# Ten long and three short token blocks instead of twelve long ones, with the freed rooms given to expert weights

## The chip, the cores and the metric

The kernel runs on one core of one Trainium2 chip. The metric is device time in microseconds (us) of one execution. Memory sizes here are in KB and MB of 1024; the profile's MB and GB/s are decimal.

## What is computed

The reference chains three parts over 4608 tokens (8 sequences of 576, 512 features): a retention attention (causal scores with a decay per head, no softmax), a gated feed-forward layer and a soft mixture of experts with 32 slots.

```python
scores = scale * q @ k.T                      # per batch and head
x = ((scores * Dmat) @ v)                     # tokens x 512
h = x @ w_in                                  # 512 -> 2048
x = (h * sigmoid(1.702 * h)) @ w_out          # 2048 -> 512
logits = x @ phi                              # 32 slots
d = softmax(logits, over tokens)
slot_input = d.T @ x                          # 8 experts x 4 slots
slot_out[e] = relu(slot_input[e] @ w1[e]) @ w2[e]
out = softmax(logits, over slots) @ slot_out
```

w1 and w2 are 16 MB each.

## The kernel before

**Blocks.** The tokens come in 36 chunks of 128. Attention makes one chunk per step (`step_of`, steps 0 to 35). Everything behind it works on blocks of NB = 384 tokens, three steps each: 12 blocks, 0 to 11. The attention output x of a block is held as two float32r halves (a high part made by ScalarE in `x_high`, a low part made by GpSimd in `x_low`).

**One block.** For each of 16 groups fc of 128 hidden channels, `expert_scores` (L368) makes hp with 12 matmuls: four pieces of 128 features, three products of halves each, a 128x128 weight load before each. ScalarE applies the gate (`gelu`, L378) into gT, which keeps four groups per tile in a ring of three tiles in `gate_room`. w_out is never applied to tokens: the logits come from gT and Wp = w_out @ phi, four groups at a time (`logits_group`, L419, Lg), and the slot sums collect d.T @ gT. For these the gates must have tokens on the partitions: VectorE transposes 32x32 pieces into `pre` (`turn_fc`, L394), and 16 DMAs per half block move them into `nat` (`shuffle`, L412), 96 KB each in runs of 1 KB. The softmax over tokens is kept up from block to block: `softmax_split`, `softmax_exp` (with the matmul lt, L432), `softmax_turn` (dp, L461) and `slots_part` (Sg, L479) for block n run inside block n+1, at the groups that tables like EXP_AT name.

**The last blocks.** Block 10 (`early`) runs the last three attention steps at its groups 0, 3 and 6. Then the attention's memory is closed and becomes the pool `pw2`. Block 11 (LAST) has no block behind it: its gates are turned by TensorE (`last_turn`, L401, tpg) and copied to `nat`, without DMAs, and its softmax runs in `tail()` in one serial chain. At its group 1 an exponential and four VectorE sums finish the softmax over slots for all earlier tokens (`combine_part`).

**The tail.** After the last slot sum, w_out is applied to the 32 slots (si_ps, L682), then the first expert layer (h_ps, L710), the second (so_ps, L753 and L761), and the results are made, copied out and written (op, L787; copies L796; DMA L797), 9 MB in 12 DMAs.

**The weights' plan.** `prefetch(place)` takes the next unit of w_out (4 MB), w1 and w2 (less 1.5 MB that are kept from early on), 34.5 MB in all, and issues its load into a room of 1 MB (or 0.5 MB) whose old content is no longer needed. In block 10 it fills 1 MB of `ring` (group 2), 4 MB of `pw2` (group 6) and at the end 1.5 MB each of x and pre; in block 11 each pair of used input weights (1 MB, every second group) and some more; in the tail and in the expert layers whatever comes free (`refill`). All DMAs, loads, shuffles and results, are issued in program order by SP, on one queue; an issue that has to wait holds all behind it. The order of each engine's work is the order of the program (`manual_schedule`).

Of the kernel before, what the change touches and what calls it, by code (L numbers as in the profile page):

```python
# [31 lines left out]
NBLK = NT // NB  # L32
LAST = NBLK - 1
# [5 lines left out]
NW2 = 4  # L39
# [6 lines left out]
STEPS = NB // CP  # L46
# [87 lines left out]
def tile_kernel(ctx, tc, qkv, w_in, w_turned, w_out, phi, w1, w2, consts, out):  # L134
# [818 lines left out]
```

## Time and profile before

| | |
|---|---|
| time, median of 3 runs | 649.25 us (648.83 to 650.72) |
| the profiled execution | 650.49 us |
| its span, first to last instruction | 648.6 us |
| mean granted TensorE clock | 0.994 of full speed |
| TensorE matmuls, busy | 626.7 us, 97% |
| moved by DMA | 150.64 MB, mean 232 GB/s |

The profile is that of one execution; all its times are inside the span, which starts with the first instruction. PE is TensorE, PEld its weight loads, DVE VectorE, ACT ScalarE, POOL GpSimd, SP the engine that issues the DMAs. L368 is line 368 of the kernel. The ends of matmuls are modelled, so a busy TensorE need not be at its peak rate; the starts are measured.

### The profile page before, as it was taken

The page shows a single profiled execution, that of the slowest core. Times are in us where ns is not written, and L with a number is a line of the kernel's source. Part 1 is how long each engine was busy: PE and PEld are TensorE (multiplying, and loading weights), DVE is VectorE, ACT ScalarE, POOL GpSimd, SP SyncE. Part 2 cuts the span into 40 slices and gives each one's busy share as a digit, 9 for nine tenths or more (in the row PEclk, how much of TensorE's full clock was granted, in tenths as well). Part 3 has the DMA queues.
Part 4 walks back from the last instruction along what each step waited for, and adds up shares of the span by engine and source line. Part 5 has one row for each costly group of instructions (what it writes and reads, how often), then busy time and mean ns, then how long its engine had stood idle before and what let it go on. Part 6 is the DMA issues. An engine that isn't in the chain of part 4 may idle for free.

```text
span 648.6 us, 19162 instructions
## 1 busy us (share of the span) xinstructions
PE 626.7 (97%) x8439; PEld 538.0 (83%) x8439; DVE 293.8 (45%) x581; ACT 216.7 (33%) x409; POOL 77.6 (12%) x70
## 2 busy tenths in 40 slices
PE   6999999999999999999999999999999999999994
PEld 6898788898998989989989979989898798874562
DVE  4989933364453443454534534544535323123043
ACT  2765432141242232422412412412424224231042
POOL 2011101211112101121111011111121100001000
PEclk9999999999999999999999999999999999999997
DMA  8997657687676756746657657566566777999998
GB/s 337 404 329 267 256 109 218 164 215 187 174 265 165 195 187 163 211 141 180 172 163 182 183 145 187 170 158 179 179 176 190 251 204 209 413 361 421 412 414 353
DMA packets 62546, 150.64 MB, mean 232 GB/s; under 512 B 8192, under 2 KB 42368, under 8 KB 53248
## 3 DMA queue, kind: packets, MB, share of 16 engines
q1 hardware_dynamic: 62464, 149.43, 72.8%
q8 instruction: 66, 1.08, 0.7%
q14 instruction: 16, 0.13, 0.1%
HBM read 101.16 MB, written 13.63 MB: 177 GB/s over the span
## 4 chain that ended last, share of the span: by engine, by line
PE 87%; DMA 6%; DVE 3%; ACT 1%; issue 1%; POOL 0%; SPq 0%; DVEq 0%; ACTq 0%
PE hp L368 56%; PE Lg L419 5%; PE Sg L479 4%; PE Sp L227 4%; PE St L227 4%; DMA early_raw<-in_moe_w_in_dram 3%; PE Op L227 2%; PE h_ps L710 2%; PE op L787 2%; PE so_ps L761 1%; DMA early_raw<-in_w_turned_dram 1%; PE so_ps L753 1%; DMA ring<-in_w_turned_dram 1%; DMA pack<-in_qkv_dram 1%; PE tpg L401 1%
## 5 line engine op out<-in xcount | busy, mean ns | idle before, releaser
L368 PE MATMUL hp<-x,w 128*128 128x384 f32 x2304 | 420.0, 339 | 1.6 <-POOL x L257 1.3
L368 PEld LDWEIGHTS hp<-x,w 128*128 128x128 f32 x2304 | 397.4, 188 | 20.2 <-issue 15.7
L394 DVE STREAM_TRANSPOSE pre<-gT 128x384 f32<-128x384 f32 x172 | 95.3, 569 | 165.5 <-ACT gT L378 154.5
L378 ACT ACTIVATE gT<-hp 128x384 f32<-128x384 f32 x188 | 91.1, 490 | 232.6 <-PE hp L368 232.2
L257 POOL TENSOR_TENSOR x<-xs,x 128x512 fp32r<-128x512 f32 x33 | 42.5, 1288 | 310.6 <-ACT x L252 310.6
L227 PE MATMUL Op<-pack 64*64 64x64 f32 x2176 | 71.8, 220 | 0.2 <-issue 0.2
L227 PEld LDWEIGHTS Op<-pack 64*64 64x64 f32 x2176 | 66.8, 135 | 0.6 <-issue 0.6
L252 ACT CAST x<-xs 128x512 fp32r<-128x512 f32 x36 | 22.3, 620 | 87.5 <-DVE xs L245 87.4
L233 POOL TENSOR_TENSOR pack<-pack,cs 128x512 f32<-128x512 f32 x30 | 32.2, 1072 | 126.9 <-DMA pack<-in_qkv_dram 111.3
L227 PE MATMUL Sp<-pack 64*64 64x64 f32 x1152 | 41.3, 222 | 5.6 <-DMA pack<-in_qkv_dram 5.5
L227 PEld LDWEIGHTS Sp<-pack 64*64 64x64 f32 x1152 | 37.8, 138 | 8.1 <-DMA pack<-in_qkv_dram 5.5
L237 DVE TENSOR_TENSOR pack<-Sp,cs 128x512 f32<-128x512 f32 x36 | 24.7, 686 | 33.5 <-PE Op L227 25.8
L227 PEld LDWEIGHTS St<-pack 64*64 64x64 f32 x1024 | 33.2, 137 | 7.4 <-issue 7.3
L227 PE MATMUL St<-pack 64*64 64x64 f32 x1024 | 37.4, 224 | 0.0
L419 PE MATMUL Lg<-gT,Wp 128*32 128x384 f32 x376 | 36.3, 493 | 0.5 <-DVE Lall L466 0.5
L479 PE MATMUL Sg<-nat,dn 128*32 128x512 f32 x264 | 30.4, 593 | 0.0
L245 DVE TENSOR_TENSOR xs<-Op,cs 128x512 f32<-128x512 f32 x36 | 24.5, 681 | 3.1 <-PE Op L227 3.1
L241 DVE TENSOR_TENSOR pack<-St,cs 128x512 f32<-128x512 f32 x32 | 21.8, 680 | 3.4 <-PE St L227 2.0
L304 ACT ACTIVATE early_raw<-early_raw 128x512 f32<-128x512 f32 x28 | 18.9, 685 | 12.3 <-DMA early_raw<-in_moe_w_in_dram 6.3
L479 PEld LDWEIGHTS Sg<-nat,dn 128*32 128x32 f32 x264 | 8.4, 110 | 17.1 <-issue 16.9
L485 DVE SCALAR_TENSOR_TENSOR acc<-acc,corr,Sg 128x512 f32<-128x512 f32 x10 | 7.5, 748 | 28.1 <-PE Sg L479 28.1
L419 PEld LDWEIGHTS Lg<-gT,Wp 128*32 128x32 f32 x376 | 9.6, 109 | 11.9 <-issue 9.1
(142 smaller groups left out, 386.8 us busy)
## 6 DMA issues: line engine op xcount, KB each, us to landing
pack<-in_qkv_dram SPq DMA_DIRECT2D x36, 1024.0 KB, 6.2
nat<-pre SPq DMA_DIRECT2D x352, 96.0 KB, 2.2
wx<-in_moe_w_dram SPq DMA_DIRECT2D x19, 1024.0 KB, 11.2
ring<-in_moe_w_out_dram SPq DMA_DIRECT2D x16, 512.0 KB, 4.0
early_raw<-in_moe_w_in_dram SPq DMA_DIRECT2D x15, 512.0 KB, 6.7
early_raw<-in_w_turned_dram SPq DMA_DIRECT2D x13, 512.0 KB, 6.9
wx<-in_moe_w_dram SPq DMA_DIRECT2D x11, 512.0 KB, 10.1
out_dram<-wx SPq DMA_DIRECT2D x5, 1024.0 KB, 7.5
```

The costliest lines, as they stand in the source:

```text
L227: pe.matmul(o[oh, p, j, :], w[h, a, p, j], w[h, b, p, j], start=first_, stop=True, skip_group_check=True)
L233: (dve if n in (3, 4) else pool).tensor_tensor(k, k, by_state(ksc[:, n % NPB, :]), op=ALU.mult)
L237: dve.tensor_tensor(packs[n][:, SC], Sps.pop(n), across(dtab), op=ALU.mult)
L241: dve.tensor_tensor(packs[n][:, SS], St[n // NPB], by_state(stsc[:, n % NPB, :]), op=ALU.mult)
L245: dve.tensor_tensor(xss[g], Ops.pop(g), across(osc), op=ALU.mult)
L252: act.copy(xh[b_][:, :, i * CP:(i + 1) * CP], xss[g].rearrange("p a j c -> p a (j c)"))
L257: (eng or pool).tensor_tensor(xl[b_][:, :, cols_], xss.pop(g).rearrange("p a j c -> p a (j c)"), xh[b_][:, :, cols_], op=ALU.subtract)
L368: pe.matmul(hp, wt[fc][:, a, dc, :], b[n][:, dc, :], start=(i == 0), stop=(i == 3 * NDC - 1))
L378: act.activation(gT[n, g][:, fl, :], hps.pop((n, fc)), AF.Gelu_apprx_sigmoid)
L394: dve.transpose(pre[n, hf][:, :, :, fh, :].rearrange("p c b i -> p (c b) i"), gT[n, g][:, fl, :].rearrange("p (x j) -> p x j", j=32))
L419: pe.matmul(Lg[n][32 * fl:32 * fl + 32, :], Wp[:, g * GF + fl, :], gT[n, g][:, fl, :], start=(g == 0), stop=(g == NFC // GF - 1))
L479: pe.matmul(Sg[32 * b:32 * b + 32], dn[n][:, c, :], nv[:, 4 * b:4 * b + 4], start=(c == 0), stop=(c == NT128 - 1))
```

## The change

Blocks 0 to 9 stay at 384 tokens; the last 768 tokens are cut into three blocks of 256 (10, 11 and LAST = 12) instead of two of 384. With them:

- Block 10 is now the `early` one and is short; its attention steps stand at groups 0, 4 and 8. The x of step 32 is made one step later, and that of steps 34 and 35 after the attention is closed, in a room of `pw2` (which has three weight rooms now, not four); until then their raw values lie in `gate_room`, of which short blocks use 3072 of 4608 columns.
- In the short blocks VectorE turns the gates late, from group 10 on, and all 16 groups go through one shuffle at the block's end, with runs of 2 KB and 128 KB per DMA, behind the weight loads issued there.
- Expert weights are loaded into the third of `pre` that short blocks don't use (group 2 of block 10), the free third of `gate_room` (end of block 10), the x of block 11 (its end), all of `pre_room` (group 7 of the last block) and the free part of `nat` (group 10). The old loads into `pre` at the end of block 10 and in block 11 are gone.
- In the last block the exponential for the slots stays at group 1, and the sums behind it (`combine_rest`) follow the softmax turn. In block 2's first group the eight matmuls with the high half of x stand first.

```diff
 NP = H // 2
 NB = 384
 NT128 = NB // 128
-NBLK = NT // NB
-LAST = NBLK - 1
+NLONG = 10
...
 GF = 4
 HF = NFC // 2
 NQ = 4
 DQ = DM // NQ
...
 NSTEP = NT // CP
-STEPS = NB // CP
+NSHORT = 2
+NBLK = NLONG + (NSTEP - NLONG * NT128) // NSHORT
+LAST = NBLK - 1
 PC = NP * CP
...
-EARLY_STEP_AT = {0: 0, 3: 1, 6: 2}
-EARLY_LOGITS_AT = {0: ((1, 2), (1, 3)), 8: ((0, 0), (0, 1))}
-EARLY_SPLIT_AT, EARLY_EXP_AT, EARLY_TURN_AT, EARLY_SLOTS_AT = 0, 1, 3, 8
+EARLY_STEP_AT = {0: 0, 4: 1, 8: 2}
+EARLY_LOGITS_AT = {0: ((1, 2), (1, 3)), 9: ((0, 0), (0, 1))}
+EARLY_SPLIT_AT, EARLY_EXP_AT, EARLY_TURN_AT, EARLY_SLOTS_AT = 0, 1, 4, 12
+SHORT_LOGITS_AT = {0: ((1, 2), (1, 3)), 9: ((0, 0), (0, 1))}
+SHORT_TURNS = {10: (0, 1, 2, 3), 11: (4, 5, 6, 7), 12: (8, 9), 13: (10, 11, 12), 14: (13, 14), 15: (15,)}
 LATE_TURNS = {**{fc: () for fc in range(4)}, 4: (0, 1), 5: (2, 3), 6: (4, 5), 7: (6, 7)}
-LAST_LOGITS = {0: ((1, 2), (1, 3)), 4: ((0, 0),), 8: ((0, 1),), 12: ((0, 2),)}
-LAST_TURNS = {6: (0, 1), 7: (2, 3), 8: (4, 5), 9: (6, 7), 10: (8,), 11: (9,), 12: (10,), 13: (11,)}
-LAST_EXP_AT, LAST_TURN_AT, LAST_SLOTS_AT = 1, 3, 6
+LAST_LOGITS = {0: ((1, 2), (1, 3)), 6: ((0, 0),), 9: ((0, 1),), 13: ((0, 2),)}
+LAST_TURNS = {4: (0,), 5: (1,), 6: (2, 3), 7: (4,), 8: (5,), 9: (6, 7), 11: (8, 9), 12: (10,), 13: (11,), 14: (12,)}
+LAST_EXP_AT, LAST_TURN_AT, LAST_SLOTS_AT = 1, 4, 10
 LAST_ACT = (0, 2, 4, 6, 8, 11, 13)
-NPRE = NTILE - 2 * NT128
+NPRE = NTILE - 2 * NSHORT
+
+
+
+def chunks_of(n):
+    return NT128 if n < NLONG else NSHORT
+
+
+def first_step(n):
+    return NT128 * n if n < NLONG else NT128 * NLONG + NSHORT * (n - NLONG)
+
+
+def block_of(g):
+    return max(n for n in range(NBLK) if first_step(n) <= g)
...
-    packs[2] = pb.tile([128, 6, NP, NSEQ, C], F32, tag="pre", name="pack2", bufs=2)
+    pre_room = pb.tile([128, 6 * 1024], F32, name="pre_room")
+    packs[2] = pre_room[:, 0:3072].rearrange("p (c a j d) -> p c a j d", c=6, a=NP, j=NSEQ)
...
     def scale_out(g):
-        xss[g] = pa.tile([128, NP, NSEQ, C], F32, tag="xs", name="xs")
+        if block_of(g) == LAST:
+            room = gate_room[:, 3072 + 512 * (g - first_step(LAST)):][:, :512]
+            xss[g] = room.rearrange("p (a j c) -> p a j c", a=NP, j=NSEQ)
+        else:
+            xss[g] = pa.tile([128, NP, NSEQ, C], F32, tag="xs", name="xs")
         dve.tensor_tensor(xss[g], Ops.pop(g), across(osc), op=ALU.mult)
 
+    def x_of(g):
+        n = block_of(g)
+        if n not in xt:
+            if n == LAST:
+                xt[n] = pw2.tile([128, 2, NDC, NSHORT * CP], F32R, tag="x", name="x", bufs=1)
+            else:
+                xt[n] = (pg if n % 2 else pb).tile([128, 2, NDC, NB], F32R, tag="x", name="x", bufs=1)
+        i = g - first_step(n)
+        return [xt[n][:, a, :, i * CP:(i + 1) * CP] for a in range(2)]
...
+        if first_step(NLONG + 1) < g < first_step(LAST):
+            x_high(g - 1)
+            x_low(g - 1)
         scale_out(g)
-        x_high(g)
-        x_low(g)
+        if first_step(NLONG + 1) != g < first_step(LAST):
+            x_high(g)
+            x_low(g)
         if g + 2 < NSTEP:
             load_step(g + 2)
...
-    def gate():
-        return gate_room[:, GF * NB * (next(gates) % 3):][:, :GF * NB].rearrange("p (l t) -> p l t", l=GF)
+    def gate(n):
+        w = GF * CP * chunks_of(n)
+        return gate_room[:, w * (next(gates) % 3):][:, :w].rearrange("p (l t) -> p l t", l=GF)
 
     def expert_scores(n, fc):
-        hp = hps[n, fc] = ps.tile([128, NB], F32, tag="h", name="hp", bufs=3)
-        i = 0
-        for dc in range(NDC):
-            for a, b in ((0, xh), (0, xl), (1, xh)):
-                pe.matmul(hp, wt[fc][:, a, dc, :], b[n][:, dc, :], start=(i == 0), stop=(i == 3 * NDC - 1))
-                i += 1
+        hp = hps[n, fc] = ps.tile([128, NB], F32, tag="h", name="hp", bufs=3)[:, 0:CP * chunks_of(n)]
+        terms = [(a, b, dc) for dc in range(NDC) for a, b in ((0, 0), (0, 1), (1, 0))]
+        if fc == 0 and n == 2:
+            terms.sort(key=lambda t: t[0] + 2 * t[1])
+        for i, (a, b, dc) in enumerate(terms):
+            pe.matmul(hp, wt[fc][:, a, dc, :], xt[n][:, b, dc, 0:CP * chunks_of(n)], start=(i == 0), stop=(i == 3 * NDC - 1))
...
+    def last_half(fc):
+        room = nat[LAST][:, (4096, 0)[fc // HF]:][:, :2048]
+        return room.rearrange("p (c a f i) -> p c a f i", c=NSHORT, a=4, f=HF)
+
+    def nat_of(n):
+        if n not in nat:
+            if n <= NLONG:
+                nat[n] = pm.tile([128, 6 * 1024], F32, tag="nat", name="nat")
+            else:
+                nat[n] = nat[NLONG]
+        k = chunks_of(n)
+        return nat[n][:, 0:2048 * k].rearrange("p (c a f i) -> p c a f i", c=k, a=4, f=NFC)
+
+    def pre_of(n, hf):
+        if n < NLONG:
+            room, f = pre_room[:, 3072 * (1 - hf):][:, :3072], HF
+        else:
+            room, f = pre_room[:, 0:2048 * NSHORT], NFC
+        return room.rearrange("p (c b f i) -> p c b f i", b=4, f=f, i=32)
...
     def shuffle(n, hf, rows=range(4)):
-        if n not in nat:
-            nat[n] = pm.tile([128, NT128, 4, NFC, 32], F32, tag="nat", name="nat")
+        to, of = nat_of(n), pre_of(n, hf)
+        fs = slice(hf * HF, (hf + 1) * HF) if n < NLONG else slice(0, NFC)
         for a in rows:
             for b in range(4):
-                sp.dma_start(nat[n][32 * b:32 * b + 32, :, a, hf * HF:(hf + 1) * HF, :],
-                             pre[n, hf][32 * a:32 * a + 32, :, b])
+                sp.dma_start(to[32 * b:32 * b + 32, :, a, fs, :], of[32 * a:32 * a + 32, :, b])
 
...
-        prefetch_three(pg.tile([128, 3, 1024], F32, tag="x", name="wx", bufs=1), 2)
-        prefetch(lambda: gate_room[:, 2560:])
-        halves = [gate_room[:, 1024:1536], acc]
-        dp = ps.tile([128, NT128, 128], F32, tag="L", name="dp")
-        for c in range(NT128):
+        prefetch(lambda: pw2.tile([128, 2048], F32, tag="x", name="wx", bufs=1))
...
-        free = [nat[n][:, c].rearrange("p a f i -> p (a f i)") for c in range(NT128)]
-        for c in range(NT128 - 1):
-            prefetch(lambda c=c: free[c])
-        prefetch(lambda: free[NT128 - 1][:, 1024:], 1)
+        for o in (0, 4096, 5120):
+            prefetch(lambda o=o: nat[n][:, o:o + 1024], 1)
...
-            early = n == LAST - 1
+            early, short = n == NLONG, n > NLONG
             step_at, logits_at, split_at, exp_at, turn_at, slots_at = (
                 (EARLY_STEP_AT, EARLY_LOGITS_AT, EARLY_SPLIT_AT, EARLY_EXP_AT, EARLY_TURN_AT, EARLY_SLOTS_AT) if early else
-                (STEP_AT if n < LAST - 2 else BEFORE_EARLY_STEP_AT, LOGITS_AT, SPLIT_AT, EXP_AT, TURN_AT, SLOTS_AT))
+                ({}, SHORT_LOGITS_AT, EARLY_SPLIT_AT, EARLY_EXP_AT, EARLY_TURN_AT, EARLY_SLOTS_AT) if short else
+                (STEP_AT if n < NLONG - 1 else BEFORE_EARLY_STEP_AT, LOGITS_AT, SPLIT_AT, EXP_AT, TURN_AT, SLOTS_AT))
             for fc in range(NFC):
                 main_fc(n, fc)
-                for f in LATE_TURNS.get(fc, (fc,)) if n == 2 else (fc,):
+                for f in LATE_TURNS.get(fc, (fc,)) if n == 2 else SHORT_TURNS.get(fc, ()) if n >= NLONG else (fc,):
                     turn_fc(n, f)
...
                 if fc in step_at:
-                    step_of((n + 1) * STEPS + step_at[fc], between)
+                    step_of(NT128 * (n + 1) + step_at[fc], between)
                 else:
                     between()
-                if fc == (0 if early else min(step_at)) and (early or n == 2):
+                if (fc == 0 and early) or (n == 2 and fc == min(step_at)):
                     shuffle(n - 1, 1)
                 if early and fc == 2:
                     prefetch(lambda: ring_raw[:, 0:4].rearrange("p a f -> p (a f)"))
+                    prefetch(lambda: pre_room[:, 4096:6144])
                 if early and fc == max(step_at):
                     att_ctx.close()
                     pw2 = ctx.enter_context(tc.tile_pool(name="pw2", bufs=NW2, side="right", reuse_waits="tile"))
                     for _ in range(NW2):
                         prefetch(place_in(pw2, "w", NW2))
+                    for g in range(first_step(LAST), NSTEP):
+                        x_high(g)
+                        x_low(g)
                 if fc == slots_at:
                     slots_part(n - 1)
-                    shuffle(n, 0)
+                    if not (early or short):
+                        shuffle(n, 0)
                 if fc == exp_at:
                     softmax_exp(n - 1)
                 if fc == turn_at:
                     softmax_turn(n - 1)
-                if fc == NFC - 1 and not early:
-                    if n < LAST - 2:
-                        shuffle(n, 1)
-                if fc == NFC - 1 and early:
-                    prefetch_three(pb.tile([128, 3, 1024], F32, tag="x", name="wx", bufs=1), 2)
+                if fc == NFC - 1 and n < NLONG - 1:
                     shuffle(n, 1)
-                    prefetch_three(pb.tile([128, 3, 1024], F32, tag="pre", name="wx", bufs=2), 0)
+                if fc == NFC - 1 and n >= NLONG:
+                    prefetch_three((pg if n % 2 else pb).tile([128, 3, 1024], F32, tag="x", name="wx", bufs=1), 2)
+                    if early:
+                        prefetch(lambda: gate_room[:, 3072:4096], 1)
+                    shuffle(n, 0)
                 if n == 3 and fc == 0:
                     for unit, a in zip(kept, (4, 8)):
                         load_unit(unit, lambda a=a, n=len(unit): ring_raw[:, a:a + 2 * n].rearrange("p a f -> p (a f)"))
@@ -884,24 +927,27 @@
                 softmax_split(n - 1)
             if fc == LAST_EXP_AT:
                 softmax_exp(n - 1)
-                combine_part(0, NPRE)
+                act.activation(Lall[:, 0:NPRE], Lall[:, 0:NPRE], AF.Exp)
             if fc == LAST_TURN_AT:
                 softmax_turn(n - 1)
+                combine_rest(0, NPRE)
             if fc == LAST_SLOTS_AT:
                 slots_part(n - 1)
-            if fc == 5:
-                prefetch_three(pb.tile([128, 3, 1024], F32, tag="pre", name="wx", bufs=2), 0, lone=True)
+                prefetch(lambda: nat[LAST][:, 2048:4096])
             for f in LAST_TURNS.get(fc, ()):
                 turn_fc(n, f)
-            if fc == 13:
-                prefetch(lambda: gate_room[:, 1536:2560], 1)
             if fc == 0:
-                prefetch(place_in(pw, "w1", 2, 1), 1)
+                prefetch(place_in(pw, "w1", 2, 1), 1, True)
             elif fc % 2 == 0:
                 prefetch(place_in(pw, "w", NFC // 2 - 1))
             if fc == GF:
-                gate()
-                prefetch(lambda: gate_room[:, 0:1024], 1)
+                gate(n)
+                prefetch(lambda: gate_room[:, 1024:2048], 1)
+            if fc == 7:
+                for i in range(2):
+                    prefetch(lambda i=i: pre_room[:, 2048 * i:2048 * i + 2048])
+            if fc == 14:
+                prefetch(lambda: gate_room[:, 2048:3072], 1)
         tail()
```

## Rows read from the trace of the kernel before

**Rows 1.** The page: busy engines, slices of the span, one instruction group, one DMA issue.
```profile
PE 626.7 (97%) x8439; PEld 538.0 (83%) x8439; DVE 293.8 (45%) x581; ACT 216.7 (33%) x409; POOL 77.6 (12%) x70
...
DMA  8997657687676756746657657566566777999998
GB/s 337 404 329 267 256 109 218 164 215 187 174 265 165 195 187 163 211 141 180 172 163 182 183 145 187 170 158 179 179 176 190 251 204 209 413 361 421 412 414 353
...
L394 DVE STREAM_TRANSPOSE pre<-gT 128x384 f32<-128x384 f32 x172 | 95.3, 569 | 165.5 <-ACT gT L378 154.5
...
nat<-pre SPq DMA_DIRECT2D x352, 96.0 KB, 2.2
```
**Rows 2.** The chain that ended last, 478 to 500 (start, length in us, what).
```profile
479.99 8.52 PE hp L368 x48
...
494.63 4.17 PE hp L368 x24
```
**Rows 3.** The same chain, 500 to the end.
```profile
513.93 1.43 PE Lg L419 x16
515.36 2.57 PE Sg L479 x24
517.93 16.86 PE hp L368 x96
...
551.20 2.71 PE Sg L479 x24
...
556.81 0.66 PE tpg L401 x6
...
559.55 0.78 PE Lg L419 x8
...
579.08 1.16 PE Lg L419 x8
...
580.26 0.57 DVE Lp L614
...
584.42 2.83 PE Sg L648 x24
...
607.05 1.01 PE hT_ps L716 x8
```
**Rows 4.** Stages: busy us of each engine, granted clock, DMA share, GB/s.
```profile
486.40:505.00 18.60, 18.60 (x349) 16.96 (x348) 10.05 (x22) 7.97 (x14) 3.62 (x3) 1.00 0.64 180
...
549.00:560.00 11.00, 11.00 (x81) 8.07 (x79) 1.86 (x3) 2.67 (x6) 0.00 (x0) 1.00 0.94 359
...
575.00:585.00 10.00, 8.77 (x58) 6.27 (x60) 3.74 (x12) 4.36 (x11) 0.00 (x0) 1.00 0.92 326
...
600.00:625.00 25.00, 25.00 (x372) 13.62 (x364) 4.01 (x14) 4.50 (x10) 0.00 (x0) 1.00 1.01 413
625.00:640.00 15.00, 13.97 (x240) 9.69 (x236) 8.50 (x16) 8.25 (x22) 0.00 (x0) 1.00 1.01 412
640.00:648.60 8.60, 0.02 (x1) 0.00 (x0) 0.59 (x3) 0.27 (x2) 0.00 (x0) 0.55 0.74 303
```
**Rows 5.** Timeline of SP's DMA issues, 486 to 562.
```profile
491.08 13.30 SPq L412 DMA_DIRECT2D nat<-pre  x16
...
533.94 13.22 SPq L412 DMA_DIRECT2D nat<-pre  x16
```
**Rows 6.** The same timeline, 600 to the end.
```profile
638.95 1.64 SPq L797 DMA_DIRECT2D out_dram<-nat  x2
640.69 1.14 SPq L797 DMA_DIRECT2D out_dram<-wx  x1
```
**Rows 7.** What the DMA engines moved from 549 to the end.
```profile
DMA packets 6784, 38.93 MB, mean 389 GB/s; under 512 B 754, under 2 KB 760, under 8 KB 3064
```
**Rows 8.** TensorE's waits, whole span (us in total, times, longest).
```profile
PE Lg L419 <- DVE Lall L466: 0.5, 1, 0.5
```
**Rows 9.** TensorE's waits, 100 to 125.
```profile
PE hp L368 <- POOL x L257: 0.4, 1, 0.4
```

More of the change, by code (lines that the diff above doesn't have):

```diff
@@ L38 @@
 HF = NFC // 2
-NW2 = 4
+NW2 = 3
 NQ = 4
@@ L398, in last_turn @@
         g, fl = divmod(fc, GF)
-        tp = ps.tile([128, NT128, 4, 32], F32, tag=tag, name="tpg", bufs=3)
-        for c in range(NT128):
+        tp = ps.tile([128, NT128, 4, 32], F32, tag=tag, name="tpg", bufs=3)[:, 0:NSHORT]
+        for c in range(NSHORT):
             pe.transpose(tp[:, c].rearrange("p a i -> p (a i)"), gT[n, g][:, fl, c * 128:(c + 1) * 128], ident)
@@ L485, in slots_part @@
             dve.scalar_tensor_tensor(acc, acc, st["corr"], sg, op0=ALU.mult, op1=ALU.add)
-    def combine_part(t0, t1):
-        L = Lall[:, t0:t1]
-        act.activation(L, L, AF.Exp)
-        combine_rest(t0, t1)
     def combine_rest(t0, t1):
@@ L613, in tail @@
         lg = Lg.pop(n)
-        dve.tensor_copy(Lp[:, 0], lg)
+        dve.tensor_copy(Lp[:, 0, 0:w], lg)
         turn_fc(n, 13)
-        lt = ps.tile([128, NB], F32, tag="L", name="lt")
-        pe.matmul(lt, sum4, Lp[:, 0], start=True, stop=True)
+        lt = ps.tile([128, NB], F32, tag="L", name="lt")[:, 0:w]
+        pe.matmul(lt, sum4, Lp[:, 0, 0:w], start=True, stop=True)
         late = {fc: last_turn(n, fc, "h") for fc in (14, 15)}
@@ L625, in tail @@
         dve.reduce_max(mb, lt, axis=AX.X)
-        act.copy(Lp[0:NS, 1], lt[0:NS])
+        act.copy(Lp[0:NS, 1, 0:w], lt[0:NS])
         dve.tensor_tensor(mnew, mb, st["m"], op=ALU.max)
         dve.tensor_scalar(negm, mnew, -1.0, None, op0=ALU.mult)
-        dr = ps.tile([128, NT128, NS], F32, tag="St", name="dr")
-        for c in range(NT128):
+        dr = ps.tile([128, NT128, NS], F32, tag="St", name="dr")[:, 0:k]
+        for c in range(k):
             pe.transpose(dr[:, c, :], Lp[0:NS, 1, c * 128:(c + 1) * 128], ident[0:NS, 0:NS])
@@ L640, in tail @@
-        for c in range(NT128):
+        prefetch(lambda: pw2.tile([128, 2048], F32, tag="x", name="wx", bufs=1))
+        prefetch(lambda: gate_room[:, 0:1024], 1)
+        halves = [gate_room[:, 4096:4608], acc]
+        dp = ps.tile([128, NT128, 128], F32, tag="L", name="dp")[:, 0:k]
+        for c in range(k):
             pe.transpose(dp[:, c, :], dT[:, c * 128:(c + 1) * 128], ident)
-        dn_ = pm.tile([128, NT128, NS], F32, tag="dn", name="dn")
+        dn_ = pm.tile([128, NT128, NS], F32, tag="dn", name="dn")[:, 0:k]
@@ L643, in tail @@
         dve.tensor_copy(dn_, dp[:, :, 0:NS])
         Sg = ps.tile([128, 4, 4, 32], F32, tag="r", name="Sg", bufs=3)
-        for c in range(NT128):
-            nv = nat[n][:, c].rearrange("p a f i -> p f a i")
+        for c in range(k):
             for b in range(4):
-                pe.matmul(Sg[32 * b:32 * b + 32], dn_[:, c, :], nv[:, 4 * b:4 * b + 4],
-                          start=(c == 0), stop=(c == NT128 - 1))
-        mx = pm.tile([128, NT128], F32, tag="mx", name="mx")
+                nv = last_half(4 * b)[:, c].rearrange("p a f i -> p f a i")
+                pe.matmul(Sg[32 * b:32 * b + 32], dn_[:, c, :], nv[:, 4 * (b % 2):4 * (b % 2) + 4],
+                          start=(c == 0), stop=(c == k - 1))
@@ L668, in tail @@
         NCT = cT[0].shape[1]
-        si_flat = free[NT128 - 1][:, 0:NE * (NDC * NS + SE)]
+        si_flat = nat[n][:, 1024:1024 + NE * (NDC * NS + SE)]
         pool.memset(si_flat[:, 0:NE * NDC * NS], 0.0)
```

66 lines of the change are left out of this document (28 added, 38 removed).

## The prediction

> **What bounds the kernel now.** I read the page first [rows 1]: TensorE is busy 97% of the span, and from slice 34 on the DMA engines are full as well, at 353 to 421 GB/s, where they move 107 to 270 before. So two things can set the end. The chain that ended last, read in two stretches [rows 2, 3], is TensorE throughout: groups of 12 expert matmuls (hp, one per 128 hidden channels), logits (Lg), slot sums (Sg), and from 579.08 us a serial tail in which a 384-wide softmax is passed between engines. [...] SP's own timeline and the DMA list [rows 5 to 7] then say what the DMA engines do: after 549.0 they move 38.93 MB. That is 27.5 of the 34.5 MB of weights that the plan holds (7 were issued by then), 9 MB of results and a rest, in 99.6 us. At the 0.415 MB/us of the full stretches this is 93.8 us; the other 5.8 are lost in 549-560 (1.5), 575-585 (2.1) and the run-out after 640 (2.3) [rows 4]. The queue is one line, so the results, the last of them issued at 640.7, wait behind the last weights. TensorE alone would end nearly as soon: from 638.95 SP still issues 2.25 MB [rows 6], and with an empty queue these need 5.6 us and about 1.5 to land (a 96 KB transfer takes 2.2 in all [rows 1]), 646.1, plus what follows the last landing. A DMA queue that is early can give at most 1.2 us; one that is late is paid in full.
>
> **The price of a short matmul.** [...] From the load's side: six 128-column loads with their transposes take 0.66 us, 110 each, and eight loads with only 32 columns to move 1.01 us, 126 each [rows 3]. [...]
>
> **TensorE's chain, part by part**, from block 10's start (486.4: 479.99 plus 36 of 48 matmuls [rows 2]) to the end.
> - Two blocks of 384 have 384 pairs, 66.7 us; three of 256 have 576, 69.4: **+2.7** (115.9: 0.0; 126: +5.9).
> - The last block turns its gates on TensorE, now two chunks for three: 13 groups before the tail, one 0.11 us transpose less in each [rows 3]: **-1.4**.
> - Logits cost 1.43 us for 16 matmuls together and 0.78 for 8 [rows 3]; by columns plus the start, 1.0 and 0.55. Before: three times 1.43 and three times 0.78; after: 1.43, four times 1.0, three times 0.55: **+0.5**.
> - Slot sums go by chunks, whose number stays 36; but a 2.57 us one [rows 3] and two of 1.8 now lie before the tail, where there were two of 2.57 and 2.71: **+0.9**. A third softmax before the tail adds 0.3 of small matmuls and 0.5 of switches: **+0.8**.
> - In the last block the sums over finished tokens (combine_rest) move behind the turn of the softmax, which had held TensorE 0.5 us; the shorter groups leave ScalarE's table switches less cover (three groups are now 4.3 us, not 6.3), and I give back 0.3: **-0.2**. In block 2 the matmuls with the low half go last, which covers a 0.4 us wait for GpSimd [rows 8, 9]: **-0.4**.
> - The tail shrinks from 384 to 256 columns: slot sum 2.83 to 1.97, the logits 1.16 to 0.9, and the other five steps of 0.5 to 0.9 us between 580.26 and 584.42 by a fifth to a quarter each, 0.75 in all [rows 3]: **-1.9**.
> Sum **+0.9**. Bunched transposes on VectorE (45% busy in all) and the later split of steps 32, 34 and 35 cost nothing: each still precedes its use by several groups; without that cover a transposition is about 0.4 us (0.57 at 384 [rows 1]).
>
> **The DMA queue.** Up to the end of block 11 the new order issues rooms of 1 + 1 + 3 + 1.5 + 0.5 = 7 MB, so 27.5 are still to come, as many as the old one had left at 549.0 [rows 7]. The question is when the rest begins to flow.
> - Block 10 took 46.3 us (486.4 to 532.7, the second being 517.93 plus 84 of 96 matmuls [rows 3]). With 16 groups of 1.446 for 2.086 and 0.4 less for logits it takes 35.7. Block 11 has no attention steps (6.1), shorter logits, slot sum and turns (1.4): 28.1. With block 2's 0.4 it ends at 549.8.
> - During block 11 no room comes free: what was issued at block 10's end (2 MB, and the shuffle) is done some 12 us later, and the engines stand nearly empty for some 15 us.
> - Only after its last matmul SP can issue 1.5 MB into x and then the shuffle of block 11, 16 DMAs of 128 KB, an extra one: the old order shuffled nothing after 549. A shuffle's price: 486.4-505 holds 0.64 x 18.6 = 11.9 us of DMA time, of which one 1 MB pack is 2.5, so 9.4 us for 16 DMAs with runs of 1 KB [rows 4, 5]. Now there are two thirds as many runs, of 2 KB: by runs 6.3 us, by bytes 5.1, by DMAs 9.4; I take 6.3, as 1 KB runs moved far below the full rate. SP's issue took 13.2 to 13.3 us for 16, waits included [rows 5]; 0.5 over the DMA time is my allowance, up to 3.
> - So weights flow again from 549.8 + 0.4 (SP's waits) + 3.8 + 6.3 + 0.5 = 560.8. Left are 26 MB of weights and 9 of results, with 0.1 of instructions 36.8 million bytes: 88.7 us, and the run-out 2.3: **651.8**. Before it was 648.6: **+3.2**. The extra rooms (pre_room, nat) keep the queue full from there, which is why the 3.6 us lost in 549-585 are not lost again; this is already in the sum.
> By TensorE alone the end would be 646.1 + 0.9 and what follows the landing, earlier than that; so the queue decides, +3.2. The sum stands against the profiled execution (650.49 us, 1.9 around its span), which lies 1.2 over the median 649.25; I add it to the median: **652.5 us**. Bounds: the shuffle by bytes and no allowance +1.5; 115.9 ns per pair takes 1.8 off block 11's end; SP at its old 13.3 us +5.9; 126 ns another 2.1.
>
> **The rivals.** About 0.3% (1.95 us) is what a measurement of this kernel can tell from no change: slower begins at 651.2, faster at 647.3.
> - *The queue is no later, TensorE decides.* If SP gets the weights in flight by 558 (short shuffle, a pair near 117), the queue ends as before or earlier, and the chain's +0.9 less at most 1.2 of queue leaves about 649. For it: DMA time falls by some 6 us in all with the larger runs. Against: the hole in block 11 is longer than that.
> - *Faster.* The weight load alone sets a short pair, 110 ns, as the transposes have it [rows 3]: the matmuls take 63.4 us, -3.3, the chain is -5.1, block 11 ends at 545.8, and with the shuffle at 5.1 and no allowance the flow starts at 555.1: the queue ends at 646.1, TensorE earlier, so 646.7. It decides from a flow before 556 on. [...]
> - *The load is no longer hidden.* At 126 ns the chain is +4.1 and the flow starts 2.1 later: queue +5.3, 654.6.
>
> **How the numbers follow.** The queue late as worked out 0.48 (0.42 over 651.2, 0.06 below it); TensorE decides, 0.22; faster 0.17; load exposed 0.13. So faster 0.17, within 0.28, slower 0.55. The likeliest case alone reaches from 650 to 655.5. The range of 8 in 10 takes in the no-change case and most of the faster one: 646.5 to 655.5.
>
> **What would show it.** After: hp groups of 12 at 1.45 us in blocks 10 to 12 (1.39 or 1.51 for the bounds); DMA nearly idle for 15 us before block 11's end; SP's first weights of the last block near 560; the share full from there to the end; the last weight landing near 628, 3 us later than before, while TensorE's last matmul moves by about one. Wrong it would be if the queue runs dry before the results, if the hole is filled, or if pairs come at 110.

## The result and the profile after

The changed kernel takes 659.05 us (median of 5 runs, 657.39 to 660.05), the one before 649.25 (648.83 to 650.72): ratio 1.0144, 95% interval 1.0124 to 1.0164, 9.4 us of 649. It is slower, as forecast, but by three times the 3.2 us that I worked out, and outside the range. The profiled execution took 659.09, its span 657.3, 8.7 more than before.

The page after, busy engines and slices; it answers to [rows 1].
```profile
PE 629.4 (96%) x8648; PEld 540.9 (82%) x8648; DVE 297.5 (45%) x607; ACT 222.2 (34%) x431; POOL 77.2 (12%) x70
...
PEclk9999999999999999999999999999999999999977
DMA  8987657786786647667566568476568775999998
GB/s 319 402 328 268 254 126 198 193 216 160 184 295 177 183 147 186 176 166 179 175 152 180 167 157 223 160 183 182 149 182 228 282 189 149 297 421 413 416 419 353
```
TensorE is busy 2.7 us longer, but its share of the span falls to 96%. The chain that ended last, 515 to the end, in place of [rows 3]:
```profile
544.68 5.83 PE hp L400 x48
...
581.01 1.17 PE Lg L466 x8
...
585.63 1.99 PE Sg L687 x16
...
588.83 15.13 DMA nat<-in_moe_w_dram
...
604.02 15.19 DMA wx<-in_moe_w_dram
...
619.27 14.98 DMA pre_room<-in_moe_w_dram
...
634.29 1.08 PE so_ps L798 x16
...
644.37 3.13 PE op L824 x26
```
48 short pairs take 5.83 us, 121.5 ns each. From 588.8 on three loads lie on the chain, each 15 us from issue to landing: that is the length of the queue, not of a load (1 MB takes 2.5 us at 415 GB/s). The stages, against [rows 4]; the last three columns are the granted clock, the DMA share (above 1 it means full) and GB/s:
```profile
534.00:549.00 15.00, 15.00 (x134) 12.71 (x133) 6.03 (x16) 3.08 (x8) 0.00 (x0) 1.00 0.32 70
549.00:556.00 7.00, 7.00 (x67) 6.28 (x67) 1.94 (x7) 3.94 (x9) 0.00 (x0) 1.00 0.81 260
556.00:562.00 6.00, 5.77 (x52) 5.12 (x51) 4.10 (x9) 3.70 (x8) 0.00 (x0) 1.00 1.05 222
562.00:566.00 4.00, 4.00 (x37) 3.86 (x34) 0.42 (x1) 1.19 (x5) 0.00 (x0) 1.00 0.71 158
566.00:575.00 9.00, 9.00 (x79) 6.88 (x78) 2.02 (x4) 2.19 (x6) 0.00 (x0) 1.00 0.99 381
...
600.00:625.00 25.00, 23.69 (x348) 12.84 (x340) 3.54 (x12) 4.07 (x8) 0.00 (x0) 1.00 1.02 415
625.00:640.00 15.00, 10.71 (x174) 6.78 (x178) 4.17 (x10) 4.12 (x12) 0.00 (x0) 0.77 1.02 420
640.00:657.30 17.30, 6.96 (x102) 5.01 (x94) 5.41 (x12) 4.83 (x13) 0.00 (x0) 0.75 0.86 357
```
The hole of block 11 is there (0.32 from 534 to 549). Behind it comes the row to look at: from 556 to 562 the DMA engines are full (1.05) and move only 222 GB/s, where weights move at 415 to 420. That is block 11's shuffle. Only from 566 on do weights flow. SP's issues say the same, against [rows 5, 6]: the shuffle takes it from 550.04 for 14.06 us, and the next weights are issued at 564.21.
```profile
522.88 14.49 SPq L460 DMA_DIRECT2D nat<-pre_room  x16
549.14 0.81 SPq L562 DMA_DIRECT2D wx<-in_moe_w_dram  x2
550.04 14.06 SPq L460 DMA_DIRECT2D nat<-pre_room  x16
564.21 1.49 SPq L562 DMA_DIRECT2D wx<-in_moe_w_dram  x3
...
619.27 0.33 SPq L562 DMA_DIRECT2D pre_room<-in_moe_w_dram  x1
```
Two waits on TensorE are new; the granted clock falls at the time of the longer one (its mean is 0.77 of full speed from 625 to 640):
```profile
PE so_ps L798 <- DMA pre_room<-in_moe_w_dram: 4.3, 1, 4.3
PE so_ps L798 <- DMA wx<-in_moe_w_dram: 1.3, 1, 1.3
```

### The profile page after: what moved, and what is told of

The parts are those of the page before. It is cut to its first block, busy times and chain, and to the rows that moved or that the text cites. A ratio compares the mean times of both kernels' runs of the same rounds, so it can differ in the third digit from the quotient of the medians.

```text
span 657.3 us, 19648 instructions
## 1 busy us (share of the span) xinstructions
PE 629.4 (96%) x8648; PEld 540.9 (82%) x8648; DVE 297.5 (45%) x607; ACT 222.2 (34%) x431; POOL 77.2 (12%) x70
## 4 chain that ended last, share of the span: by engine, by line
PE 81%; DMA 12%; DVE 3%; ACT 1%; issue 1%; POOL 0%; SPq 0%; DVEq 0%; ACTq 0%
PE hp L400 57%; PE Lg L466 5%; PE Sg L523 5%; PE St L245 4%; PE Sp L245 4%; DMA early_raw<-in_moe_w_in_dram 4%; PE Op L245 3%; DMA wx<-in_moe_w_dram 2%; DMA nat<-in_moe_w_dram 2%; DMA pre_room<-in_moe_w_dram 2%; DMA early_raw<-in_w_turned_dram 1%; PE op L824 1%; PE so_ps L798 1%; DMA pack<-in_qkv_dram 1%; DVE w L357 1%
## 5 line engine op out<-in xcount | busy, mean ns | idle before, releaser
L400 PE MATMUL hp<-x,w 128*128 128x384 f32 (+1 forms) x2496 | 422.9, 327 | 1.5 <-POOL x L284 0.7
L409 ACT ACTIVATE gT<-hp 128x384 f32<-128x384 f32 (+1 forms) x204 | 93.7, 466 | 238.0 <-PE hp L400 237.5
L442 DVE STREAM_TRANSPOSE pre_room<-gT 128x384 f32<-128x384 f32 (+1 forms) x188 | 97.8, 542 | 157.6 <-ACT gT L409 139.1
L284 POOL TENSOR_TENSOR x<-xs,x 128x512 fp32r<-128x512 f32 x31 | 40.0, 1290 | 281.4 <-ACT x L280 281.4
L245 PE MATMUL Op<-pack 64*64 64x64 f32 x2112 | 70.1, 221 | 0.5 <-issue 0.5
L245 PEld LDWEIGHTS Op<-pack 64*64 64x64 f32 x2112 | 65.2, 135 | 0.8 <-issue 0.7
L251 POOL TENSOR_TENSOR pack<-pack,cs 128x512 f32<-128x512 f32 x29 | 30.7, 1060 | 139.5 <-DMA pack<-in_qkv_dram 133.5
L466 PE MATMUL Lg<-gT,Wp 128*32 128x384 f32 (+1 forms) x408 | 36.9, 468 | 0.9 <-DVE Wp L370 0.9
```

The lines of the kernel that those rows point to most:

```text
L245: pe.matmul(o[oh, p, j, :], w[h, a, p, j], w[h, b, p, j], start=first_, stop=True, skip_group_check=True)
L251: (dve if n in (3, 4) else pool).tensor_tensor(k, k, by_state(ksc[:, n % NPB, :]), op=ALU.mult)
L284: (eng or pool).tensor_tensor(xl, xss.pop(g).rearrange("p a j c -> p a (j c)"), xh, op=ALU.subtract)
L400: pe.matmul(hp, wt[fc][:, a, dc, :], xt[n][:, b, dc, 0:CP * chunks_of(n)], start=(i == 0), stop=(i == 3 * NDC - 1))
L409: act.activation(gT[n, g][:, fl, :], hps.pop((n, fc)), AF.Gelu_apprx_sigmoid)
L442: dve.transpose(pre_of(n, hf)[:, :, :, fh if n < NLONG else fc, :].rearrange("p c b i -> p (c b) i"), gT[n, g][:, fl, :].rearrange("p (x j ...
```

## Experiments

Three theories. **1**: the end is set by when weights flow again behind block 11's shuffle. **2**: short matmuls and TensorE's added work set it. **3**: the last weight unit comes last but is used second in the last quarter of the output; this wait and the lower clock after it set the end. Each run was timed beside the kernel before, and ratios are to that. The profiles differ by up to 3.6 us in when block 10 ends, which has nothing to do with the edits, so I also give the **rest**: the span less the time at which SP starts block 10's shuffle. For the changed kernel it is 657.3 - 522.88 = 134.4 us. A rest comes from one profile. The two pairs of runs below that differ least (e6 and e6b, e7 and e7b) have rests 0.4 and 1.4 us apart, so a difference of about 1 us in it is not shown by itself.

**Without the shuffle (e1).** The last block's slot sums then use gates that were never moved.
```
-                    shuffle(n, 0)
+                    if early:
+                        shuffle(n, 0)
```


> Leaves out the shuffle of block 11's gates (its 16 DMAs), so the last block's slot sums use gates that were never moved. Theory 1 (the end is set by when weights flow again behind that shuffle on the DMA queue): the last weight's issue moves from 619.3 us to about 605 and the kernel gains 8 to 10 us against the changed kernel, to about 649 to 651, until TensorE's chain decides. Theory 2 (256-column matmuls and TensorE's added work set the end): no change, 658 to 660. Theory 3 (the order of the last weight units, with the drop of the clock after it, sets the end): 2 to 4 us less at most, as far as the wait for them shrinks.

650.97 us, ratio 1.0014 (0.9998 to 1.0029), rest 126.3: nearly the whole loss is gone, 8.1 us by the rest. The last weight is issued at 609.0 for 619.3; I had said about 605. Theory 2 falls, since every short matmul is still there.

**Where TensorE alone would end (e9).** As e1, with `turn_fc` of block 11 left out and the two 1 MB rooms of `pre_room` loaded behind block 10's shuffle.

> Where TensorE's chain alone would end: the changed kernel without block 11's transposition and shuffle (both left out, so the last slot sums read block 10's gates), and with 2 MB of weights loaded into the room of the transposed gates in the hole of block 11, from 540 us on. TensorE's work is that of the changed kernel. If the change costs TensorE the 0.9 us that the prediction worked out and the DMA queue alone makes the rest: the DMA engines are no longer full at the end, and the time is 645 to 648, a little below that of the run without the shuffle. If TensorE's chain sets the end already there: no change against that run, 650 to 651.

650.91 us, ratio 1.0001 (0.9984 to 1.0018), rest 126.6: the second case. 2 MB loaded earlier bring nothing, and the engines have slack (share 0.64, windows of this run):
```profile
566.00:575.00 9.00, 9.00 (x79) 6.88 (x78) 1.60 (x3) 2.17 (x6) 0.00 (x0) 1.00 0.64 226
```
TensorE waits for no DMA in e1 and e9. Its last matmuls, in the kernel before, in e1 and in e9 (start and length):
```profile
636.39 3.13 PE op L787 x26
```
```profile
635.40 3.13 PE op L824 x26
```
```profile
638.68 3.13 PE op L824 x26
```
From block 10's first matmul (at 486.27, 484.01 and 487.51) TensorE's chain takes 153.2, 154.5 and 154.3 us. So e1 and e9 end with TensorE's chain, which the change made 1.1 to 1.3 us longer behind that point; by the ratio, e9 lies within -1.0 and +1.2 us of the kernel before. In these three traces the DMA engines are full from 600 to 640 (share 1.01) and the span ends 9.1 to 9.5 us behind TensorE; what a faster TensorE would gain is not shown.

**The order of the last weights (e2).**
```
-        def second_layer(q, e):
+        def second_layer(q, e, last=NE - 1):
...
-                          start=(e == 0 and f < 4), stop=(e == NE - 1 and f >= 4))
+                          start=(e == 0 and f < 4), stop=(e == last and f >= 4))
...
-        for e in range(NE):
-            second_layer(3, e)
+        for e, x in enumerate((0, 2, 3, 4, 5, 6, 7, 1)):
+            second_layer(3, x, 1)
```


> The changed kernel with the experts of the last quarter of the output in the order 0, 2, 3, 4, 5, 6, 7, 1, so that the weight unit that is loaded last is used last. Theory 1 (the DMA queue decides, and TensorE's 5.6 us of waits for weights and its lower clock behind them are hidden by the results still queued): 0 to -1 us, 658 to 659. Theory 3 (these waits and the clock set the end): -4 to -6 us, 653 to 655. Theory 2: no change.

657.47 us, ratio 1.0117 (1.0099 to 1.0136), rest 134.5, as without the edit (by the ratios 1.8 us less). The windows of this run:
```profile
634.00:640.00 6.00, 4.91 (x58) 3.48 (x46) 3.65 (x8) 3.54 (x11) 0.00 (x0) 1.00 1.03 426
640.00:645.00 5.00, 0.00 (x0) 0.00 (x0) 0.50 (x3) 0.23 (x2) 0.00 (x0) 0.62 1.01 423
645.00:655.00 10.00, 0.00 (x0) 0.00 (x0) 0.00 (x0) 0.00 (x0) 0.00 (x0) 0.50 0.82 340
```
TensorE is done by 640, at full clock; in the changed kernel it was 647.5 (644.37 and 3.13). Block 10 ends 1.7 us earlier in this profile, so the order gains TensorE about 6 us. The DMA engines still move results for 15 us, and the end stays. Theory 3 falls.

**Delay alone, in the kernel before (e3).**
```
             if fc == 0:
+                more = pd.tile([4, 128, 2, EF], F32, name="more")
+                for i in range(4):
+                    sp.dma_start(more[i], w1[i, 0])
                 prefetch(place_in(pw, "w1", 2, 1), 1)
```


> The kernel before, with 4 MB of copies from HBM to HBM put on SP's queue just ahead of the last block's first weights; nothing of the computation is left out, and TensorE's work is that of the kernel before. Theory 1: a delay of the DMA flow alone makes the loss of the change: 4 MB cost 8 to 10 us (at 2.4 us per MB, less about 1 us that the queue was early; more if a copy costs a read and a write), 657 to 660. Theory 2: the queue has slack, at most +2 us.

659.97 us, ratio 1.0156 (1.0134 to 1.0177): 10.1 us, 2.5 for each MB. The same waits of TensorE appear here, without one short matmul:
```profile
PE so_ps L761 <- DMA wx<-in_moe_w_dram: 6.9, 4, 4.3
```

**The price of the shuffle: half the bytes (e4), twice the DMAs (e8).**
```
-                sp.dma_start(to[32 * b:32 * b + 32, :, a, fs, :], of[32 * a:32 * a + 32, :, b])
+                cs_ = slice(0, 1) if n == NLONG + 1 else slice(0, chunks_of(n))
+                sp.dma_start(to[32 * b:32 * b + 32, cs_, a, fs, :], of[32 * a:32 * a + 32, cs_, b])
```
e8 instead issues one such DMA for each chunk `c`. e4 leaves the second chunk's gates unmoved.

> The changed kernel with only the first of block 11's two 128-token chunks shuffled: 16 DMAs of 64 KB for 16 of 128 KB (the second chunk's gates are not moved, so part of the last slot sums is wrong). Theory 1 with the price by bytes or runs: half of the gain of leaving the shuffle out, 4 to 5 us, 654 to 655. Theory 1 with the price by DMAs (SP's issue and its waits for landings): nearly no gain, 0 to 2 us. Theory 2: no change.

> The changed kernel with block 11's shuffle cut into 32 DMAs of 64 KB for 16 of 128 KB (the same bytes in the same runs of 2 KB); nothing is left out. If the shuffle is paid by the DMA (0.63 us of SP's issue each): the weights of the last block start about 10 us later and the kernel is 8 to 10 us slower than the changed kernel, 667 to 669. If it is paid by bytes or runs: 0 to 1 us slower, 659 to 660.

e4: 657.55 us, ratio 1.0109 (1.0091 to 1.0126), rest 133.7, only 0.7 less (2.3 by the ratios). e8: 668.95 us, ratio 1.0286 (1.0264 to 1.0308), rest 143.9, 9.4 more. SP's issues in e4, and then in e8:
```profile
549.62 13.30 SPq L461 DMA_DIRECT2D nat<-pre_room  x16
```
```profile
549.71 23.38 SPq L461 DMA_DIRECT2D nat<-pre_room  x32
```
Windows of e4:
```profile
556.00:562.00 6.00, 5.77 (x52) 4.99 (x51) 3.80 (x8) 3.40 (x8) 0.00 (x0) 1.00 0.35 81
```
With half the bytes the engines are a third busy and SP takes nearly as long as ever; e8 has 16 more DMAs of the same 64 KB than e4, and they cost 10.1 us of SP, 0.63 each. So at 64 KB a DMA costs its issue, and SP's issue alone keeps 7.4 of the 8.1 us that e1 gave back. At 128 KB both limits meet: SP's 14.1 us, and 2.1 MB / 0.222 = 9.4 us of DMA time behind 3.8 for x. These two runs can't tell whether the DMA time alone would be enough there.

**Another queue (e5), two queues (e12).**
```
-                sp.dma_start(to[32 * b:32 * b + 32, :, a, fs, :], of[32 * a:32 * a + 32, :, b])
+                (pool if n == NLONG + 1 and b % 2 else sp).dma_start(
+                    to[32 * b:32 * b + 32, :, a, fs, :], of[32 * a:32 * a + 32, :, b])
```
is e12; e5 is without `and b % 2`.

> The changed kernel with block 11's 16 shuffle DMAs issued from GpSimd's queue instead of SP's, so that SP may issue the last block's weights from 549.5 us on, beside them; nothing is left out. If SP's own issue and its waits for landings hold the flow (14 us for 16 DMAs while the DMA engines could do more): 4 to 6 us faster than the changed kernel, 653 to 655. If the DMA engines' time is what the shuffle costs (9.4 us for 16 DMAs with runs of 2 KB, whoever issues them): only the gaps of 562 to 568 us come back, 1 to 2 us, 657 to 658.

> The changed kernel with block 11's 16 shuffle DMAs split between two queues, 8 on SP's and 8 on GpSimd's, so that issuing them takes half the time and the weights follow 8 of them; nothing is left out. If SP's issue alone held the flow and the DMA engines could move the 2.1 MB at the 0.415 MB/us of weights (5 us): 4 to 6 us faster than the changed kernel, 653 to 655. If the DMA engines need 9.4 us for it whoever issues (0.222 MB/us at a full share): only the gaps come back, 1 to 2 us, 657 to 658; with TensorE waiting for the later half as in the run on GpSimd's queue alone, no gain or a loss.

e5: 665.82 us, ratio 1.0239 (1.0204 to 1.0274), rest 141.2: neither case. Weights are issued on SP's queue beside the shuffle (seven loads from 550.18 to 563.04), the DMA engines are full (1.02 from 566 to 575), the shuffle's last DMA, issued at 571.66, lands at 582, and TensorE's slot sum waits:
```profile
PE Sg L523 <- DMA nat<-pre_room: 11.0, 1, 11.0
```
e12: 657.04 us, ratio 1.011 (1.0084 to 1.0137), rest 133.6: 0.8 us by the rest, 2.2 by the ratios. With half of the issue taken from SP the engines stay full and are still slow, although the first weights (from 559.9 on) are in this window of e12:
```profile
556.00:562.00 6.00, 5.77 (x51) 4.98 (x50) 4.22 (x9) 2.76 (x8) 0.00 (x0) 1.00 1.04 236
```
SP issues the weights 2.9 us earlier than in the changed kernel, counted from block 10's shuffle, and only 0.8 to 2.2 us come of it. So at 128 KB the DMA time alone is enough for nearly the whole price, as SP's issue alone is in e4. The two limits lie within a microsecond or two of each other, and taking one away gives back no more than that. The issues of e12, on SP's and on GpSimd's queue:
```profile
548.59 11.16 SPq L460 DMA_DIRECT2D nat<-pre_room  x8
```
```profile
549.24 4.40 POOL L460 DMA_DIRECT2D nat<-pre_room  x8 [40.63 <-PE hp L400]
```

**Why half the rate: the order of the halves (e15 on one queue, e14 on two).**
```
+        if n == NLONG + 1:
+            for a in (0, 1, 2, 3):
+                for b in (0, 1):
+                    sp.dma_start(to[32 * b:32 * b + 32, :, a, fs, :], of[32 * a:32 * a + 32, :, b])
+                    x, y = (a + 2) % 4, b + 2
+                    pool.dma_start(to[32 * y:32 * y + 32, :, x, fs, :], of[32 * x:32 * x + 32, :, y])
+            return
```
is e14; e15 issues the same pairs in the same order, both on `sp`.

> The changed kernel with block 11's 16 shuffle DMAs in another order on the same queue: each one to partitions 0 to 63 is followed by one to partitions 64 to 127 (its source likewise from the other half); nothing is left out. If the shuffle's 0.222 MB/us belong to each DMA of 32 partitions by itself, or SP's issue holds it: no change, 658 to 660. If DMAs of different halves move beside each other: up to 4 us of DMA time less, but SP's issue of 14 us keeps most of it, 657 to 658. [...]

> The changed kernel with the shuffle split between two queues by halves: SP moves to partitions 0 to 63, GpSimd's queue to 64 to 127 at the same time, and from different halves too; nothing is left out. Against the split run before, where both queues went to both halves: if the halves move beside each other, the 2.1 MB take 5 to 6 us instead of 9.4 and the kernel gains 2 to 4 us more, 653 to 655. If they don't: as that run, 656 to 658. [...]

e15: 658.65 us, ratio 1.013 (1.0108 to 1.0151), rest 134.5. e14: 657.74 us, ratio 1.0125 (1.0096 to 1.0154), rest 133.3, as e12. The windows in which SP issues nothing else, of the changed kernel and then of e15:
```profile
557.50:562.00 4.50, 4.27 (x40) 3.62 (x38) 3.80 (x8) 2.22 (x7) 0.00 (x0) 1.00 1.06 223
```
```profile
557.50:562.00 4.50, 4.28 (x38) 3.90 (x41) 3.63 (x8) 2.28 (x6) 0.00 (x0) 1.00 0.99 234
```
By share that is 210 GB/s and 236, an eighth more and far from 415. The order of the halves is a small part of it; most of the low rate stays with each of these DMAs by itself. They copy within SBUF, and between two groups of 32 partitions; no run copies within SBUF over more partitions, so which of the two makes the rate low is not shown.

**Mends with nothing left out: 1 MB into the hole (e10), with two queues (e13), with the halves (e16).**
```
...
-        room = nat[LAST][:, (4096, 0)[fc // HF]:][:, :2048]
+        room = nat[LAST][:, (0, 2048)[fc // HF]:][:, :2048]
...
                     shuffle(n, 0)
+                    if early:
+                        prefetch(lambda: nat[NLONG][:, 4096:6144])
...
-                prefetch(lambda: nat[LAST][:, 2048:4096])
...
```
The weights take the last third of `nat`; the last block's gates are turned from its group 10 on, into the two thirds that block 11's gates leave then.

> The changed kernel with 1 MB loaded in the hole of block 11 and the shuffle as it is: the last third of the token-major gates takes weights right behind block 10's shuffle (537 us), and the last block's gates are turned from its channel group 10 on into the first two thirds, which the changed kernel gave to gates and to weights; nothing is left out. Theory 1: 1 MB less behind the shuffle, 2 to 2.5 us faster than the changed kernel, 656 to 657. If the bunched transposes hold TensorE up and TensorE decides: no gain or a loss of 1 us.

> The same split of the shuffle together with the 1 MB loaded in the hole of block 11 (the last block's gates turned from its channel group 10 on); nothing is left out. If both gains are of DMA time on one queue, they add: 1 to 2 us below the run with the 1 MB alone, 653.5 to 655 where that run gave 655.5. If TensorE's wait for the later half decides: equal to that run or slower.

> The split by halves together with the 1 MB loaded in the hole of block 11 (the last block's gates turned from its channel group 10 on); nothing is left out. If the halves move beside each other: 650 to 652, as much as the whole loss back, until TensorE's chain decides. If not: as the split run with the 1 MB, 654 to 655.

e10: 655.46 us, ratio 1.0075 (1.0049 to 1.0101), rest 131.4: 3.0 less, what 1 MB costs (2.5 in e3) and a little. e13: 654.36 us, ratio 1.0067 (1.0047 to 1.0086), rest 129.8. e16: 653.83 us, ratio 1.0057 (1.0038 to 1.0077), rest 129.7. Half of the loss or more comes back. The gains seem to add; the intervals of e10, e13 and e16 overlap.

**No shuffle, block 11 turned on TensorE (e6, e6b), with 3 MB in the hole (e7, e7b).** `turn_fc` takes the last block's way for block 11 too. In e6 and e7 the ninth channel group was written over block 10's gates before block 10's slot sums read them; e6b and e7b turn it one position later.

> The changed kernel with block 11's gates turned on TensorE, as the last block's are (32 transposes of 0.11 us, 3.5 us of TensorE's time, with copies on ScalarE and VectorE), in place of 16 VectorE transposes and the 16 shuffle DMAs; every weight is loaded into the same room at the same place of the order; nothing is left out. Theory 1 (the shuffle in front of the weights is the loss): the flow starts at 549.5 us and the kernel gains 7 to 9 us, 650 to 652. Theory 2 (TensorE's work sets the end): 3 to 4 us slower, 662 to 663.

> As the run before (block 11 turned on TensorE, no shuffle of its gates), and the rooms that this frees loaded in the hole of block 11: 2 MB into the room of the transposed gates as soon as block 10's shuffle has landed (540 us), 1 MB into the middle third of the token-major gates after block 10's slot sums (543 us); nothing is left out. Theory 1: 3 MB, 7 us of DMA time, move from behind 549 us into the hole, and the queue is early enough for TensorE to decide: 645 to 648, faster than both kernels. Theory 2: as the run before or slower.

> Block 11 turned on TensorE as in the run of that kind before, with the ninth of its channel groups turned only behind block 10's slot sums (one position later), so that these sums are whole; nothing is left out. As there: 653 to 655 on TensorE's chain, which the run before showed 5 us longer than without the shuffle (32 transposes and their starts), and no DMA bound in front of it.

> The same with the ninth group behind block 10's slot sums, and 3 MB loaded in the hole of block 11; nothing is left out. Theory 1 with TensorE's chain as it stood in the run of that kind before: the DMA engines have slack in the last block, and the time is that of the run without loads in the hole, within 1 us: 653 to 656.

e6: 654.61 us, rest 130.8; e6b: 654.07 us, ratio 1.0058 (1.0036 to 1.008), rest 130.4; e7: 656.0 us, rest 131.4; e7b: 656.05 us, ratio 1.0075 (1.005 to 1.0101), rest 130.0. All lie 3.7 us or more above e1 by the rest. 3 MB in the hole bring nothing: the rest moves by less than a microsecond either way, and the ratio of e7b is the higher one. The queue is relieved (share 0.67 from 566 to 575 in e7b, below), and TensorE's transposes now set the end: from block 10's first matmul to its last one TensorE takes 3.4 us longer in e6b and e7b than in e1, and 32 transposes of 0.11 us (0.66 for 6 [rows 3]) are 3.5. I had forecast e7 below both kernels; that was wrong.
```profile
566.00:575.00 9.00, 9.00 (x80) 7.38 (x72) 2.77 (x5) 2.05 (x6) 0.00 (x0) 1.00 0.67 231
```
No version beat the kernel before: by e1 and e9 TensorE's chain ends no sooner than it did.

## Why the prediction was too small

- **Pair price**: 120.5 ns forecast, 121.5 measured (5.83 us for 48). Right. The 120.5, on which the +2.7 and the 1.446 us of a group rest, was my estimate, with a fixed part in each pair; no run shows such a part by itself. In its place the traces show 173.8 ns for a pair of 384 columns (4.17 us for 24 [rows 2]) and 121.5 for one of 256, 52.3 ns for 128 columns. The bounds, 115.9 (173.8 by columns) and 126 (eight loads of 32 columns in 1.01 us [rows 3]), hold.
- **TensorE's chain, +0.9**: from block 10 on the sum is +1.3 (the -0.4 of block 2 lies ahead of it), and e9 and e1 have +1.1 and +1.3. Right. Its last logits did not shrink as forecast (1.17 us for 0.9, and 1.16 before [rows 3]).
- **Block 11's end and the hole**: forecast 549.8; SP issues x at 549.14. Right.
- **The queue decides the end, not TensorE**: right (e1, e2, e3). From the restart to the end I had 88.7 + 2.3 = 91.0 us; the rates of 415 to 420 and the 2.4 us lost after 640 (17.3 us at a share of 0.86) bear both terms out.
- **The step that failed is the price of the shuffle** ("by runs 6.3 us, by bytes 5.1, by DMAs 9.4; I take 6.3") with its 0.5 for SP. I had weights flow again 11.0 us after block 11's end. Going back 91.0 us from the end of the span gives 566.3, 17.2 after it. The last weight says the same: it lands at 634.25 (619.27 and 14.98), 6.2 us behind the 628 that I named. Counted as DMA time, of the 6.2 us more 3.1 are the shuffle's (9.4 for 6.3). Another 1.3 are gaps: 0.81 x 7 + 1.05 x 6 + 0.71 x 4 = 14.8 us busy of 17, 2.2 idle where I allowed 0.9. The last 1.8 I can't split; they lie in 549 to 575, where weights and shuffle mix and move less than 415 GB/s. Counted as SP's issue (14.06 us from 550.04 on), the weights are issued at 564.21, 15.1 us after block 11's end. The two counts overlap: in e4 the shuffle needs 4.7 us of DMA time, less than my 6.3, and still 7.4 of 8.1 us are lost. So the 0.5 for SP failed as much as the 6.3, and a right DMA price alone would not have put the forecast right.

The 9.4 that I named and passed over was this number, for a wrong reason. I had taken it for the price of the old shuffle, by subtracting one pack from a window with other transfers in it [rows 4], and had then scaled by the number of runs. Windows of the kernel before in which shuffle DMAs stand all but alone (16 of 96 KB, issued by SP from 517.99 on) were there to be read:
```profile
526.00:530.00 4.00, 4.00 (x25) 4.00 (x24) 1.16 (x2) 0.98 (x2) 0.00 (x0) 1.00 0.38 83
530.00:534.00 4.00, 4.00 (x25) 4.00 (x24) 1.16 (x2) 0.98 (x2) 0.00 (x0) 1.00 0.76 155
```
GB/s by share: 83 / 0.38 = 218 and 155 / 0.76 = 204, for runs of 1 KB. Runs of 2 KB go at 222 / 1.05 = 211. The length of a run does not matter here, so the price goes by bytes at about 0.21 MB/us, half of what weights get: 2.1 MB take 10 us. With 10 for 6.3 the forecast would have been 656.2. The bound that I gave for SP's old 13.3 us (+5.9, the whole move against the kernel before) gives 655.2. Neither alone reaches the 659.05, which has both and the gaps between them.
- **"TensorE's last matmul moves by about one"**: wrong, it moved from 639.5 to 647.5, by the waits for late weights. I did not ask which late unit is needed first. It cost nothing (e2), since 15 us of results were queued behind it.

## What to carry to other kernels

Price a kind of transfer by a window in which it stands alone, as GB/s divided by the DMA share (here 211 for the shuffle, where weights move 415 to 420), and by SP's issue time for each DMA (0.63 us at 64 KB in e8). Here the larger of the two counted, and where they met, taking one away gained little (by the rest 0.7 us in e4 and 0.8 in e12). A transfer put ahead of a queue that set the end cost its whole time (8.1 us by e1, 10.1 for 4 MB in e3); work moved into an earlier hole paid part of it back (3.0 us for 1 MB in e10). A wait of TensorE's, even one of 4.3 us in which its mean clock is 0.71, says nothing of the end until one looks at what is still queued elsewhere (without it the rest is 134.5 for 134.4, e2).

## What the runs showed of the hardware

- Copies from 32 partitions to 32 others move 204 to 218 GB/s, taken to a full DMA share, with runs of 1 KB (before, 526 to 534) and 210 to 211 with runs of 2 KB (the changed kernel, from 556 and from 557.5 to 562), where weights from HBM move 415 to 420 (600 to 640); with neighbouring DMAs in opposite halves of the partitions 236 (e15, 557.5 to 562).
- In e5 the shuffle stood on a second queue. Its first eight DMAs were issued in 4.39 us from 551.74 on, while SP issued loads from 550.18 on; the last, issued at 571.66, took 10.3 us to land, at 582. The last one of the changed kernel, issued at 563.5, took 3.7, to about 567.
- A shuffle DMA of 64 KB takes SP 0.63 us to issue (e8 less e4). Eight of 128 KB were issued in 4.40 us on GpSimd's queue in e12, without a wait, while SP took 11.16 for its eight behind the loads for x.
- In the changed kernel the mean granted clock was 0.71 from 630 to 634, in which TensorE waited, 0.63 from 634 to 640, when it worked again, and 1.00 from 640 to 645. In e2, without the long wait, it was 1.00 from 625 to 640, and 0.50 from 645 to 655 with TensorE done. The changed kernel's windows:
```profile
630.00:634.00 4.00, 0.00 (x1) 0.00 (x0) 0.53 (x3) 0.43 (x2) 0.00 (x0) 0.71 1.02 418
634.00:640.00 6.00, 5.71 (x86) 3.78 (x90) 0.63 (x2) 0.94 (x3) 0.00 (x0) 0.63 1.02 425
640.00:645.00 5.00, 3.97 (x78) 2.64 (x71) 2.43 (x6) 2.34 (x7) 0.00 (x0) 1.00 1.01 419
```
